# Moving GpSimd's division and the FFN layers half a step later in an attention and top-k FFN kernel

## The chip, the core and the metric

The kernel runs on one core of a Trainium2 chip. The metric is the device time of one execution in microseconds. Before the change the median of three runs is 708.19 us (706.77 to 708.98). The profile was taken in a further execution, whose span from the first to the last instruction is 704.8 us; all times within the kernel count from the start of that span.

## The reference, cut to what matters

```python
# attention: q, k, v are (8, 8, 1152, 64), float32
q_pool = q.reshape(B, H, S // 2, 2, D).mean(axis=3)          # 576 queries
scores = scale * np.matmul(q_pool, k.transpose(0, 1, 3, 2))
attn = softmax(scores)                                       # over 1152 keys
x = matmul(attn, v), heads side by side                      # (8, 576, 512)

# mixture of depths: in each batch, 128 of the 576 tokens get the FFN
scores = np.einsum('bsd,d->bs', x, w_gate)                   # the gate
out = x.copy()
for b in range(B):
    top_idx = np.argpartition(-scores[b], capacity)[:capacity]
    xe = x[b, top_idx]
    ye = np.maximum(xe @ w1, 0.0) @ w2                       # 512 -> 1024 -> 512
    g = 1.0 / (1.0 + np.exp(-scores[b, top_idx]))
    out[b, top_idx] = x[b, top_idx] + g[:, None] * ye
```

## The kernel before

The work is cut into 32 *pairs* (two heads of one batch) and each pair into two *halves* (288 of its 576 queries), so there are 64 halves, numbered 0 to 63; an even half is the first of its pair. `run` goes over the halves and emits, for each, one stretch of instructions for every engine. Each engine executes its own list strictly in the order in which it was emitted.

What one half does, engine by engine:

- TensorE (PE): `scores(h)`, 9 chunks of keys against the queries, then `weighted(h-1)`, the attention weights of the half before times v.
- ScalarE (ACT): the exponential of each chunk into `p`, the copy `two` of the weighted result, and small copies between groups of partitions.
- GpSimd (POOL): `folded` adds two thirds of `p` (three `acc` instructions), `multiplied` forms `prod` = undivided output times gate weights, `av` adds the two parts of the weighted result, `qp` pools the queries of a coming pair, and `x` is the division by the softmax sums.
- VectorE (DVE): reduces `p` and `acc` to softmax sums (`fold`, `sum`), transposes keys and queries of a coming pair (`kT`, `qT`) and the output (`avb`), takes reciprocals (`rec`), and does the ranking of the tokens.
- SyncE (SP): the loads of the coming pairs and the stores of `x`.

```python
def weighted(self, half):
    ...                                                   # 72 matmuls
    nc.scalar.copy(two[:, :, :], av[:, :, 0:n])
    nc.gpsimd.tensor_tensor(out=half["av"][:, :], in0=two[:, 0, :], in1=two[:, 1, :], op=ALU.add)

def normalized(self, pair):
    ...                                                   # for the last pair the sums are merged by TensorE
    nc.vector.reciprocal(rec[:, :], tot)
    nc.gpsimd.tensor_tensor(out=x[:, :, :], in0=pair["avb"][:, :, :], in1=rec (broadcast), op=ALU.mult)

def gated(self, half):
    nc.vector.tensor_reduce(pair["red"][:, ns], pair["prod"][:, ns, :], AX.X, ALU.add)
    if half["s"] == 1:
        nc.vector.tensor_tensor(out=pair["part"][:, pair["hp"], :], in0=pair["red"], in1=pair["rec"], op=ALU.mult)
        if pair["hp"] == self.NPAIR - 1:
            ...                                           # start the routing of this batch
```

The routing of a batch (`routed`) is a generator in pieces. A piece is emitted either in the middle of a half (`mid`, between `scores` and `weighted`) or at its end. For batch b, whose last half is 8b+7, the pieces of batches 0 to 5 lie in these halves: gate line at 8b+10, merged over partitions at 8b+11 and sent through DRAM to all partitions, ranking of the token tiles 0 and 1 at the end of 8b+13, tiles 2 and 3 at the end of 8b+14, tile 4 at the end of 8b+15, slot selection (`pick`, `index`) and the gather of 128 rows (`xe`, an indirect DMA from GpSimd) at the end of 8b+16, TensorE's transposes of `xe` (`xeT`) in the middle of 8b+18, the first FFN layer at 8b+19, the second at 8b+20, and the scatter after that. Batch 5 stops after its first layer and does the second behind the last half, as do batches 6 and 7 with more of theirs, so that TensorE has work there.

```python
for h in range(n_halves + 1):
    if h < n_halves:
        ...                                  # loads, stores
        self.scores(half)
        ...                                  # side_by_side (even) or spread (odd)
        self.units(mid=True)
        if h > 2: self.gated(halves[h - 3])
        self.folded(half)
        if h > 1: self.multiplied(halves[h - 2])
        if s == 0 and loaded: self.prepare_pair(upcoming)        # qp, kT, qT
    ...
    if h > 0:
        self.weighted(done); self.drained(done)                  # done = halves[h - 1]
    ...
    if 1 < h < n_halves and s == 0: done["pair"]["total"] = self.added(...)
    ...
    elif h > 2 and s == 1: self.normalized(halves[h - 2]["pair"])  # rec and x
    if h < n_halves: self.units(mid=False)
...                                          # behind the last half
pieces(older, self.NFC - 2)                  # older, old, new: batches 5, 6, 7
pieces(new, 1); pieces(older, 2); pieces(new, 3); pieces(older); pieces(old, self.NFC)
pieces(new, 1); ...; pieces(old, self.NFC - 3); pieces(new, 2); pieces(old); ...; pieces(new)
```

Of the kernel before, what the change touches and what calls it, by code (L numbers as in the profile page):

```python
# [10 lines left out]
P = 128  # L11
BLK = 32
# [522 lines left out]
class _Plain:  # L535
# [396 lines left out]
    def normalized(self, pair):  # L932

        nc, hp = self.nc, pair["hp"]
        tot = self.sums[:, pair["b"] * self.NPAIR + hp, :]
        if self.last_pair(pair):
            ps = self.banks()[:, 0, :]
            nc.tensor.matmul(
                ps[:, 0 : 2 * self.QB],
                lhsT=self.merge.rearrange("p g j -> p (g j)"),  # L940
                rhs=pair["sum"].rearrange("p j n -> p (j n)"),
                start=True,
                stop=True,
            )
            for j in range(2):
                rows = slice(j * self.D, (j + 1) * self.D)
                nc.scalar.activation(
                    tot[rows, :],
                    ps[rows, j * self.QB : (j + 1) * self.QB],
                    AF.Identity,  # L950
                    bias=self.tiny[rows, 0:1],
                )
        rec = pair["rec"] = self.small.tile([P, self.QB], F32, name="rec")
        nc.vector.reciprocal(rec[:, :], tot)  # L954
        x = self.work.tile([P, self.QB, BLK], F32, name="x")
        nc.gpsimd.tensor_tensor(  # L956
            out=x[:, :, :],
            in0=pair["avb"][:, :, :],
            in1=rec[:, :].unsqueeze(2).broadcast_to([P, self.QB, BLK]),
            op=ALU.mult,  # L960
        )
        pair["x"] = x

    def stored(self, pair):

# [7 lines left out]
    def gated(self, half):  # L973

        nc, pair, hb = self.nc, half["pair"], self.HB
        if half["s"] == 0:
            pair["red"] = self.small.tile([P, self.QB], F32, name="red")
        ns = slice(half["s"] * hb, (half["s"] + 1) * hb)
        nc.vector.tensor_reduce(pair["red"][:, ns], pair["prod"][:, ns, :], AX.X, ALU.add)
        if half["s"] == 1:  # L980
            nc.vector.tensor_tensor(  # L981
                out=pair["part"][:, pair["hp"], :],
                in0=pair["red"][:, :],
                in1=pair["rec"][:, :],
                op=ALU.mult,
            )
            if pair["hp"] == self.NPAIR - 1:
                unit = self.routed(pair["b"], pair["part"])
                at = next(unit) == "mid"
                self.routing.append([pair["b"], unit, at])  # L990

# [3 lines left out]
    def routed(self, b, part):  # L997
# [12 lines left out]
        sc = ffn.tile([P, NT], F32, name="gate_sc")  # L1010
        if b < self.B - 1:

            yield mid
            if b < self.B - 2:
                groups = self.side_by_side(line)
                yield True
# [19 lines left out]
                sc[0 : self.TAIL, NF:], row[NF * P :].rearrange("(t p) -> p t", p=self.TAIL)  # L1036
            )
            yield True
            if b < self.B - 2:
                yield True  # L1040
        else:

            diag = ffn.tile([P, self.QB, BLK], F32, name="diag", bufs=1)
# [34 lines left out]
        for t, rows in tiles:  # L1078
            at = t * P
            cmp = ffn.tile([P, Sp], F32, name="cmp", bufs=1)  # L1080
            own = sc[0:rows, t : t + 1]
            if t > 0:
                nc.vector.tensor_scalar(
                    out=cmp[0:rows, 0:at],
                    in0=sc_row[0:rows, 0:at],
                    scalar1=own,
                    scalar2=None,
                    op0=ALU.is_ge,
                    op1=ALU.add,
                    accum_out=parts[0:rows, t, 0:1],  # L1090
                )
            nc.vector.tensor_scalar(
                out=cmp[0:rows, at:Sp],
                in0=sc_row[0:rows, at:Sp],
                scalar1=own,
                scalar2=None,
                op0=ALU.is_gt,
                op1=ALU.add,
                accum_out=parts[0:rows, t, 1:2],
            )  # L1100
            tie = ffn.tile([P, P], F32, name="tie", bufs=1)
            nc.vector.scalar_tensor_tensor(
                out=tie[0:rows, 0:rows],
                in0=sc_row[0:rows, at : at + rows],
                scalar=own,
                in1=self.before[0:rows, 0:rows],
                op0=ALU.is_equal,
                op1=ALU.mult,
                accum_out=parts[0:rows, t, 2:3],
            )  # L1110
            if t == 1:
                yield True
            if t == 3:
                yield mid
                nc.scalar.activation(gate[:, :], gate[:, :], AF.Exp, scale=-1.0)
                if b < self.B - 2:
                    yield True
# [19 lines left out]
        for s0, w in self.slots:  # L1137
# [23 lines left out]
            else:  # L1161
# [3 lines left out]
                for of, to in ((self.token_line, found), (lines[:, :, 1, :], own_gate)):  # L1165
# [6 lines left out]
                        op1=ALU.mult,  # L1172
                        accum_out=to[0:w, :],
                    )
                nc.gpsimd.tensor_scalar(  # L1175
                    out=index[0:w, :],
                    in0=found[0:w, :],
                    scalar1=float(b * Sp),
                    scalar2=None,
                    op0=ALU.add,  # L1180
                )
            xe = ffn.tile([P, self.Dm], F32, name="xe")
            nc.gpsimd.indirect_dma_start(
                out=xe[0:w, :],
# [4 lines left out]
                oob_is_err=False,  # L1189
            )  # L1190
            yield True
            yield mid

            xeT = ffn.tile([P, self.ND, P], F32, name="xeT")
            pv = self.banks()[:, 0, :].rearrange("p (c n) -> p c n", n=P)
# [94 lines left out]
        )  # L1290
        return count_i

    def units(self, mid):


        for entry in self.routing[::-1]:
            b, unit, at = entry
            if b in self.waiting or at != mid:
                continue
            end = next((mark for mark in unit if mark), None)  # L1300
            if end is None:
                self.routing.remove(entry)
            elif end == "hidden" and b == self.B - 3:
                self.waiting.add(b)
            entry[2] = end in ("mid", "hidden") and b < self.B - 2

    def run(self):
        nc = self.nc
# [10 lines left out]
            self.load_values(loaded)  # L1319
        self.load_gate()  # L1320
        weights = self.weight_loads()
        for h in range(n_halves + 1):
            if h < n_halves:
                n, s = divmod(h, 2)
                if s == 0:
                    pair = upcoming
                    if pair["hp"] == 0:
                        part = self.ffn.tile([P, self.NPAIR, self.QB], F32, name="part")
                    pair["part"] = part
                else:  # L1330
                    loaded = None
                    if n + 2 < len(pairs):
                        loaded = self.load_pair(*pairs[n + 2])
                        self.load_values(loaded)
                    if n > 1:
                        self.stored(halves[h - 4]["pair"])
                if h > 1:
                    next(weights, None)
                half = {"pair": pair, "s": s}
                halves.append(half)  # L1340
                self.scores(half)
                if h > 1:

                    of = halves[h - 2 - s]["pair"]
                    if s == 0:
                        of["groups"] = self.side_by_side(of["sum"].rearrange("p j n -> p (j n)"))
                    else:
                        self.spread(of)
                self.units(mid=True)
                if h > 2:  # L1350
                    self.gated(halves[h - 3])
                self.folded(half)
                if h > 1:
                    self.multiplied(halves[h - 2])
                if s == 0 and loaded:
                    upcoming = loaded
                    self.prepare_pair(upcoming)
            else:
                self.stored(halves[h - 3]["pair"])
                self.gated(halves[h - 3])  # L1360
                self.multiplied(halves[h - 2])
                self.units(mid=True)
                self.units(mid=False)
            if h > 0:
                done = halves[h - 1]
                self.weighted(done)
                self.drained(done)
            if h == n_halves:
                self.multiplied(done)
                self.gated(halves[h - 2])  # L1370
            if 1 < h < n_halves and s == 0:
                done["pair"]["total"] = self.added(done["pair"]["groups"])
            if h == n_halves:
                self.normalized(done["pair"])
            elif h > 2 and s == 1:
                self.normalized(halves[h - 2]["pair"])
            if h < n_halves:
                self.units(mid=False)
        for _ in weights:
            pass  # L1380

        self.stored(halves[-1]["pair"])


        self.gated(halves[-1])
        left = [unit for _, unit, _ in self.routing]
        new = left.pop()
        old = left.pop() if left else iter(())
        older = left.pop() if left else iter(())
        assert not left  # L1390

        def pieces(unit, n=None):
            for i, _ in enumerate(unit):
                if i + 1 == n:
                    break

        pieces(older, self.NFC - 2)
        pieces(new, 1)
        pieces(older, 2)
        pieces(new, 3)  # L1400
# [71 lines left out]
```

## Time and profile before

| | value |
|---|---|
| median of 3 runs | 708.19 us (706.77 to 708.98) |
| span of the profile | 704.8 us |
| granted TensorE clock | 0.998 of full |
| score matmuls, line 818 | 4608, 295.2 us busy |
| weighted matmuls, line 836 | 4608, 294.6 us busy |
| FFN matmuls, lines 1208 and 1221 | 59.3 and 57.3 us busy |
| exponentials, line 825 | 576, 320.2 us |
| `acc` on GpSimd, line 857 | 192, 266.3 us |
| `x` on GpSimd, line 956 | 32, 37.1 us; GpSimd idle ahead of it 40.3 us |
| `part` on VectorE, line 981 | 32, 27.0 us |
| `index` on GpSimd, line 1175 | 7, 6.4 us; GpSimd idle ahead of it 20.2 us |

A group of instructions is named by its line in the program, its engine and its tile. Busy time is the time in which an engine executed; idle time ahead of a group is put down to what released it. PE is TensorE's matmuls and PEld its weight loads, which overlap.

### The profile page before, as it was taken

Reading aid. Unit: us, or ns where it says so; the run is one execution under the profiler, and the core shown is the slowest. Engines: PE = TensorE matmul, PEld = TensorE weight load, DVE = VectorE, ACT = ScalarE, POOL = GpSimd, SP = SyncE. Lnnn points to the kernel's source line nnn. Section 1 sums busy time; section 2 is a strip of 40 time slices with the busy share of each in tenths; the row PEclk is TensorE's granted clock in tenths of the full one; section 3 lists DMA queues with packets and bytes.
Section 4 is the critical chain, followed back from the end, with each engine's and each line's share of the span. In section 5 each row is a group of like instructions: output and inputs, shape, how many; then the busy total and the mean of one; then the engine's idle time right before and its main releaser. Section 6 shows DMA issues by size and latency. Waiting matters only on the chain.

```text
span 704.8 us, 23397 instructions
## 1 busy us (share of the span) xinstructions
PE 694.4 (99%) x9948; PEld 516.8 (73%) x9948; DVE 496.5 (70%) x793; ACT 444.5 (63%) x963; POOL 485.1 (69%) x452
## 2 busy tenths in 40 slices
PE   8999999999999999999999999999999999999996
PEld 5668899996758866688656887578775787766573
DVE  3877777996559965498754988559774697689540
ACT  6677778777547775477746776467754777477210
POOL 5877777868658695586955779467874877686520
PEclk9999999999999999999999999999999999999999
DMA  8888887858486483756928468382775728432200
GB/s 175 172 178 180 171 166 137 146 116 161 85 149 111 85 162 75 145 97 111 172 40 159 81 129 160 66 148 61 161 130 85 135 56 169 83 72 62 45 31 35
DMA packets 389490, 82.86 MB, mean 118 GB/s; under 512 B 376640, under 2 KB 376640, under 8 KB 389376
## 3 DMA queue, kind: packets, MB, share of 16 engines
q1 hardware_dynamic: 387872, 76.49, 58.1%
q0 software_dynamic: 1280, 4.20, 1.8%
q8 instruction: 80, 1.31, 0.8%
q10 hardware_dynamic: 224, 0.59, 0.3%
q14 instruction: 34, 0.28, 0.1%
HBM read 69.65 MB, written 11.59 MB: 115 GB/s over the span
## 4 chain that ended last, share of the span: by engine, by line
PE 89%; POOL 5%; issue 2%; DMA 1%; ACT 1%; DVE 1%; SPq 0%; POOLq 0%; DVEq 0%; ACTq 0%
PE ps L836 36%; PE ps L818 36%; PE ps L1208 8%; PE ps L1221 7%; POOL acc L857 2%; ACT p L825 1%; DMA kb<-in_k_dram 1%; DMA xe<-out_dram,index 1%; PE ps L1197 1%; POOL prod L925 1%; POOL x L956 0%; POOL av L846 0%; DVE fold L862 0%; POOL index L1175 0%; SPq L759 0%
## 5 line engine op out<-in xcount | busy, mean ns | idle before, releaser
L825 ACT ACTIVATE p<-ps 128x576 f32<-128x576 f32 x576 | 320.2, 695 | 1.7 <-PE ps L818 1.3
L818 PE MATMUL ps<-qT,kT 64*64 64x288 f32 x4608 | 295.2, 404 | 0.2 <-ACT p L825 0.2
L836 PE MATMUL ps<-p,v_sb 64*64 64x288 f32 x4608 | 294.6, 403 | 0.0
L857 POOL TENSOR_TENSOR acc<-p 128x576 f32<-128x576 f32 x192 | 266.3, 1417 | 15.4 <-ACT p L825 15.1
L836 PEld LDWEIGHTS ps<-p,v_sb 64*64 64x64 f32 x4608 | 215.5, 133 | 65.3 <-ACT p L825 9.2
L818 PEld LDWEIGHTS ps<-qT,kT 64*64 64x64 f32 x4608 | 208.0, 132 | 73.0 <-ACT p L825 15.4
L862 DVE TRANSPOSE_TENSOR_REDUCE fold<-p 128x54 f32<-128x1728 f32 x64 | 126.0, 1969 | 50.2 <-ACT p L825 50.2
L862 DVE TRANSPOSE_TENSOR_REDUCE fold<-acc 128x54 f32<-128x1728 f32 x64 | 125.3, 1957 | 46.0 <-POOL acc L857 45.8
L844 ACT COPY two<-ps 128x576 f32<-128x576 f32 x64 | 40.9, 639 | 156.9 <-PE ps L836 143.8
L846 POOL TENSOR_TENSOR av<-two 128x288 f32<-128x288 f32 x64 | 51.2, 800 | 96.5 <-ACT two L844 94.9
L915 DVE STREAM_TRANSPOSE avb<-av 128x288 f32<-128x288 f32 x64 | 29.4, 460 | 66.5 <-POOL av L846 66.5
L956 POOL TENSOR_TENSOR x<-avb,rec 128x576 f32<-128x576 f32 x32 | 37.1, 1159 | 40.3 <-DVE rec L954 27.9
L1208 PEld LDWEIGHTS ps<-xeT,w 128*128 128x128 f32 x512 | 57.8, 192 | 2.7 <-ACT p L825 2.6
L1208 PE MATMUL ps<-xeT,w 128*128 128x128 f32 x512 | 59.3, 277 | 0.0
L1221 PE MATMUL ps<-w,hT 128*128 128x512 f32 x128 | 57.3, 598 | 0.0
L925 POOL TENSOR_TENSOR prod<-avb,w_gate 128x288 f32<-128x288 f32 x64 | 51.5, 805 | 0.6 <-DVE avb L915 0.6
L902 ACT ACTIVATE sums<-total,tiny 32x18 f32<-32x18 f32 x124 | 38.1, 308 | 15.9 <-DVE total L893 14.2
L732 POOL TENSOR_TENSOR qp<-qb 128x576 f32<-128x576 f32 x31 | 43.8, 1414 | 2.2 <-DMA qb<-in_q_dram 2.2
L1221 PEld LDWEIGHTS ps<-w,hT 128*128 128x128 f32 x128 | 23.6, 190 | 28.1 <-issue 25.8
L735 DVE STREAM_TRANSPOSE kT<-kb 128x1152 f32<-128x1152 f32 x31 | 42.5, 1370 | 0.0
L887 ACT COPY groups<-sum 32x36 f32<-32x36 f32 x124 | 27.1, 219 | 6.7 <-DVE sum L872 5.2
L981 DVE TENSOR_TENSOR part<-red,rec 128x18 f32<-128x18 f32 x32 | 27.0, 845 | 1.1
(95 smaller groups left out, 290.6 us busy)
## 6 DMA issues: line engine op xcount, KB each, us to landing
kb<-in_k_dram SPq DMA_DIRECT2D x124, 144.0 KB
qb<-in_q_dram SPq DMA_DIRECT2D x124, 144.0 KB
v_sb<-in_v_dram SPq DMA_DIRECT2D x124, 144.0 KB
out_dram<-x SPq DMA_DIRECT2D x128, 72.0 KB
lines<-row_rank SPq DMA_DIRECT2D x7, 640.0 KB
w<-in_moe_w_dram SPq DMA_DIRECT2D x8, 512.0 KB
sc_row<-row SPq DMA_DIRECT2D x7, 288.0 KB
acc<-in_q_dram ACTq DMA_DIRECT2D x2, 288.0 KB
```

Source lines behind the costliest of these rows:

```text
L732: nc.gpsimd.tensor_tensor(out=qp[:, :, :], in0=pair["q"][:, :, 0, :], in1=pair["q"][:, :, 1, :], op=ALU.add)
L735: nc.vector.transpose(kT.rearrange("p (c g i) -> p c g i", c=self.NC, i=BLK), pair["k"].rearrange("p (g c) d -> p c g d", c=self.NC),)
L818: nc.tensor.matmul(sc[keys, j, 0:n], lhsT=pair["kT"][rows, c * P + keys.start : c * P + keys.stop], rhs=pair["qT"][rows, qs], start=True, ...
L825: nc.scalar.activation(p[:, c // G, c % G, :, :], sc[:, :, 0:n], AF.Exp, scale=self.scale)
L836: nc.tensor.matmul(av[j * self.D : (j + 1) * self.D, e, 0:n], lhsT=half["pair"]["v"][keys, j, c, :], rhs=half["p"][keys, c // G, c % G, j, :],
L844: nc.scalar.copy(two[:, :, :], av[:, :, 0:n])
L846: nc.gpsimd.tensor_tensor(out=half["av"][:, :], in0=two[:, 0, :], in1=two[:, 1, :], op=ALU.add)
L857: nc.gpsimd.tensor_tensor(out=acc[:, u, :], in0=units[:, 0, u, :], in1=units[:, 1, u, :], op=ALU.add)
L862: nc.vector.tensor_reduce(fold[:, a, :], of.rearrange("p u (m d) -> p (u m) d", d=BLK), AX.X, ALU.add, apply_transpose=True,)
L925: self.nc.gpsimd.tensor_tensor(out=pair["prod"][:, ns, :], in0=pair["avb"][:, ns, :], in1=self.w_gate[:, hp : hp + 1, :].broadcast_to([P, ...
L1208: nc.tensor.matmul(pv[:, f, 0:w], lhsT=self.w1[:, c, (f0 + f) * P : (f0 + f + 1) * P], rhs=xeT[:, c, 0:w], start=(c == 0), stop=(c == self ...
L1221: nc.tensor.matmul(ps[0:w, 0 : self.Dm], lhsT=hT[:, f, 0:w], rhs=self.w2[:, f, :], start=(f == 0), stop=(f == self.NFC - 1),)
```

## The change

The change moves work in time and between engines. It adds no matmul and takes none away.

1. The division `x` of a pair goes from the odd half in which its reciprocals are made to the end of the next even half (`divided`).
2. `part`, the gate sums times the reciprocals, goes from VectorE to GpSimd, except in the last two pairs of the last batch.
3. `index` goes from GpSimd to VectorE. The gather of batches 0 to 5 goes from the end of a half to a new place (`sums`) behind the `acc` instructions of the next half, and the transposes and both FFN layers follow one half later. The gate line is formed at `sums` too.
4. Batch 6: its gate line is merged in the middle of the next half, its tiles are ranked in two units (0 to 2, then 3 and 4) instead of three, its gather goes to the end of the last half, and the transposes of its rows go behind the last half.
5. `total` of an even half comes ahead of `kT` and `qT` on VectorE.
6. Behind the last half the order is new: `weighted` of the last half comes first, then the FFN of batch 5, both divisions and stores late, and the transposes of batch 6 behind five more steps of that FFN.

```diff
-        rec = pair["rec"] = self.small.tile([P, self.QB], F32, name="rec")
-        nc.vector.reciprocal(rec[:, :], tot)
-        x = self.work.tile([P, self.QB, BLK], F32, name="x")
-        nc.gpsimd.tensor_tensor(
+        pair["rec"] = self.small.tile([P, self.QB], F32, name="rec")
+        nc.vector.reciprocal(pair["rec"][:, :], tot)
+
+    def divided(self, pair):
+        x = pair["x"] = self.work.tile([P, self.QB, BLK], F32, name="x")
+        self.nc.gpsimd.tensor_tensor(
 ...
-            nc.vector.tensor_tensor(
+            ending = pair["b"] == self.B - 1 and pair["hp"] >= self.NPAIR - 2
+            engine = nc.vector if ending else nc.gpsimd
+            engine.tensor_tensor(
                 out=pair["part"][:, pair["hp"], :],
 ...
-            if t == 1:
+            cuts = (2,) if b == self.B - 2 else (1, 3)
+            if t == cuts[0] < cuts[-1]:
                 yield True
-            if t == 3:
+            if t == cuts[-1]:
                 yield mid
 ...
-                nc.gpsimd.tensor_scalar(
+                nc.vector.tensor_scalar(
                     out=index[0:w, :],
 ...
+                yield "sums" if b < self.B - 2 else True
             xe = ffn.tile([P, self.Dm], F32, name="xe")
             nc.gpsimd.indirect_dma_start(...)
             yield True
-            yield mid
+            if b < self.B - 2:
+                yield True
+            if b != self.B - 2:
+                yield mid
 ...
+            self.units("mid")
+            if h > 2:
                 self.gated(halves[h - 3])
+            self.folded(half)
+            self.units("sums")
+            if h > 1:
                 self.multiplied(halves[h - 2])
+            if h > 1 and s == 0:
+                last["total"] = self.added(last["groups"])
+            if s == 0 and loaded:
+                self.prepare_pair(upcoming)
             if h > 0:
+                self.weighted(halves[h - 1])
+                self.drained(halves[h - 1])
+            if h > 2 and s == 1:
+                self.normalized(halves[h - 2]["pair"])
+            if h > 3 and s == 0:
+                self.divided(halves[h - 3]["pair"])
+            self.units("end")
 ...
+        self.gated(halves[-3])
+        self.weighted(halves[-1])
+        self.drained(halves[-1])
+        self.multiplied(halves[-2])
+        self.multiplied(halves[-1])
+        self.gated(halves[-2])
+        pieces(older, 1)
+        self.normalized(halves[-1]["pair"])
+        for half in (halves[-3], halves[-1]):
+            self.divided(half["pair"])
+            self.stored(half["pair"])
+        self.gated(halves[-1])
+        _, new, _ = self.routing.pop()
+        pieces(new, 1)
+        pieces(older, self.NFC - 3)
+        pieces(old, 1)
         pieces(new, 1)
         pieces(older, 2)
         pieces(new, 3)
```

## The prediction, made before the result was known

> **What bounds the kernel now.** I read the page's first two parts, then TensorE's own waits, then the timeline of TensorE at the places the waits name, and last GpSimd and VectorE around those places.
>
> ```profile
> PE 694.4 (99%) x9948; PEld 516.8 (73%) x9948; DVE 496.5 (70%) x793; ACT 444.5 (63%) x963; POOL 485.1 (69%) x452
> PE   8999999999999999999999999999999999999996
> POOL 5877777868658695586955779467874877686520
> ```
>
> TensorE is busy 694.4 of 704.8 us, and the slices show where the other 10.4 us lie: in the first and in the last. No other engine passes 70%. So taking work off GpSimd or VectorE gains nothing by itself; the change can only gain where one of them makes TensorE wait. TensorE's waits, cut to the second half of the run:
>
> ```profile
> PE ps L1197 <- DMA xe<-out_dram,index: 0.6, 1, 0.6
> PE ps L1054 <- DVE rank_parts L1076: 0.4, 1, 0.4
> PE ps L1197 <- ACT p L825: 0.3, 1, 0.3
> ```
>
> They add up to 1.3 us. But busy time hides waits in a pipelined engine, so I also took the spacing between starts. A clean stretch of scores or of weighted values takes 4.37 us from its start to the start of the next. The stretch of scores ahead of the transposes (line 1197) of batches 0 to 5 takes 4.68, 4.74, 4.81, 5.33, 4.80 and 5.22 us. One of the six, in the timeline of TensorE (start, length, engine, line):
>
> ```profile
> 590.49 4.91 PE L818 MATMUL ps<-qT,kT 64*64 64x288 f32 x72
> 595.71 0.63 PE L1197 MATMUL ps<-ident,xe 128*128 128x128 f32 x4 [0.31 <-ACT p L825]
> ```
>
> A change of matmul shape costs something of itself: scores ahead of the first FFN layer (line 1208) take 4.48, so 0.11 us. Above 4.48 the six lose 0.20 + 0.26 + 0.33 + 0.85 + 0.32 + 0.74 = 2.7 us. The releaser is ScalarE: the transposes need a PSUM buffer that an exponential must first empty. In five of these six halves the copy `two` that goes ahead of the exponentials starts 0.62 to 0.77 us after the scores start, not 0.33 as elsewhere, and it starts just after GpSimd's gather instruction ends. Batch 1, in the timelines of GpSimd and ScalarE:
>
> ```profile
> 246.71 1.14 POOL L1183 DMA_INDIRECT xe<-out_dram,index  x1 [0.28 <-POOL index L1175]
> 248.16 0.64 ACT L844 COPY two<-ps 128x576 f32<-128x576 f32 x1 [2.22 <-PE ps L836]
> ```
>
> The gather ends at 247.85, `two` starts at 248.16. I don't know the mechanism; that the two belong together is my reading of a coincidence seen five times.
>
> The end, again TensorE's timeline:
>
> ```profile
> 648.00 4.59 PE L836 MATMUL ps<-p,v_sb 64*64 64x288 f32 x72
> 653.20 0.63 PE L1197 MATMUL ps<-ident,xe 128*128 128x128 f32 x4 [0.61 <-DMA xe<-out_dram,index]
> 653.76 4.59 PE L836 MATMUL ps<-p,v_sb 64*64 64x288 f32 x72
> 658.29 0.41 PE L938 MATMUL ps<-sum,merge 128*128 128x36 f32 x2
> 658.53 5.40 PE L1221 MATMUL ps<-w,hT 128*128 128x512 f32 x12
> 664.28 1.21 PE L1054 MATMUL ps<-diag,ones 128*128 128x288 f32 x4 [0.35 <-DVE rank_parts L1076]
> ```
>
> TensorE waits 0.61 us for batch 6's rows and 0.35 us for the last batch's gate line. From 664.28 on it has no gap until its last matmul at 698.2.
>
> **What the Trainium skill says.** "Perfetto Trace Analysis", section "Identifying the Most-Contended Engine", warns that busy time of pipelined matmuls is no measure of what is left. The trace agrees: 2.7 us lie in the spacing above and only 0.5 us of them show as idle time. Its section "GPSIMD Engine Instruction" advises timing GpSimd by start-to-start spacing, which I do below; the trace's `acc` at 131.09 follow each other every 4.16 / 3 = 1.39 us, against a listed mean of 1.417. "SBUF — State Buffer", section "SBUF: two separate sides", says VectorE instructions with two SBUF inputs and GpSimd exclude each other for a whole instruction. The trace agrees: the tie comparison (line 1102) lasts 271 to 1575 ns, and `part` on 18 elements takes a mean of 845 ns. So `part` costs VectorE mostly waiting, and less on GpSimd.
>
> **The change part by part.**
>
> *Removed from VectorE:* 30 of 32 `part`, 30 x 0.845 = 25 us. *Added to GpSimd:* from 805 ns for 288 elements and 1417 ns for 576, about 0.19 us plus 2.1 ns an element, so 0.23 us for 18, 30 times: 7 us. `index` takes 7 x 0.92 = 6.4 us off GpSimd. `x` no longer waits for its reciprocals (40.3 us idle ahead of it), nor `index` for `pick` (20.2 us). All of this lies beside TensorE: worth nothing directly.
>
> *The gather and the transposes.* In batches 0 to 5 the gather moves behind `acc` of half 8b+17 and the transposes to 8b+19. Rows that landed 4.9 us after the gather's start now have over 10 us, and the gather no longer lies between `weighted` and `two`. If `two` starts 0.33 us after the scores, the exponential that frees the transposes' buffer, the sixth, ends 0.33 + 0.54 + 6 x 0.545 = 4.1 us after them, before the scores end. So most of the 2.7 us goes: I take 2.2.
>
> *The end.* The transposes of batch 6 move behind 5 more FFN steps, so the last `weighted` starts at 652.4 instead of 653.76. FFN step 0 (0.86) and line 938 (0.3) follow, then 5 steps of 0.86: the transposes are due at 662.3. The gather starts when GpSimd has done `acc` of half 63 (about 653.9, below), `prod` and `av`: 655.7, and lands by 660.6. No wait. The gate line: last `two` at 656.9, `av` to 658.3, `avb`, two `prod` to 659.9 (the divisions, 1.16 us each, are no longer ahead), `red`, `part` (0.62), `line`, `diag` (0.76) at 662.2; line 1054 is due at 662.8. No wait, with 0.6 us to spare. Gain 0.61 + 0.35, plus two changes of shape of about 0.15 saved around the last `weighted` and the batch 6 merge: 1.3 us. From line 679 on the order is as before, so the gain is kept.
>
> *The new wait.* GpSimd now executes `part` of an even half ahead of `acc`, and `part` needs `red`, which stands on VectorE behind the ranking of the half before. So at halves 8b+14 and 8b+16 GpSimd can't start `acc` until the ranking is done. Batch 0, VectorE and GpSimd:
>
> ```profile
> 131.14 0.67 DVE L1092 TENSOR_SCALAR_CACHE_REDUCE cmp<-sc_row,gate_sc 128x448 f32<-128x448 f32 x1
> 131.74 0.91 DVE L1102 SCALAR_TENSOR_TENSOR tie<-sc_row,gate_sc,before 128x128 f32<-128x128 f32 x1
> 132.58 0.44 DVE L979 TENSOR_REDUCE red<-prod 128x9 f32<-128x288 f32 x1
> ...
> 131.09 4.20 POOL L857 TENSOR_TENSOR acc<-p 128x576 f32<-128x576 f32 x3
> ```
>
> Before, `acc` of half 14 started at 131.09, beside the ranking; now `part` starts at 133.1 and `acc` at 133.3, 2.2 us later. With the trace's spacings I carried this on: VectorE's second `fold` of half 14 starts at 137.5, `total` and `kT` and `qT` end at 142.1, tiles 2 and 3 (2.8 us) end at 145.1, both folds of half 15 at 149.4, tile 4 and the ranks at 151.5, `red` at 151.8, `part` and `acc` of half 16 from 151.9 to 156.2, its second `fold` to 158.3, `total`, `kT` and `qT` to 160.9. TensorE needs this `qT` at 161.96, when the scores of half 18 start. Before, it was there at 158.45. The slack falls from 3.5 to 1.1 us. It is enough, unless a tie comparison meets `acc` badly: in batch 3 one took 1.57 us instead of 0.34, which would use it up. I count 0.5 us of new waits in six batches.
>
> Sum: -2.2 - 1.3 + 0.5 = -3.0 us, 708.2 to 705.2.
>
> **Rivals.**
>
> *Hidden anyway.* TensorE is 99% busy, the long scores come from ScalarE's pace whatever GpSimd does, and one half later they are as long. For it: ScalarE needs 9 x 0.545 = 4.9 us for exponentials of scores that take 4.37, in every half. Against it: line 1208 needs a buffer in the same way and its scores take 4.48. Then only the end's 1.3 us remain: 706.9.
>
> *VectorE becomes the bound while it ranks.* If my 1.1 us of slack is 1 us too high, and ties are slow, `qT` comes up to 1.5 us late in each of six batches, at halves 18, 26, 34, 42, 50 and 58. For it: VectorE is full in these stretches (18.75 of 20 us from 140 to 160). Against it: the FFN just ahead gives it 7 us of rest in each batch. Then 6 x 1.5 = +9 less 3: 711 at worst, 708 to 709 more likely.
>
> *The end stalls on the later gather.* GpSimd's `acc` of half 63 comes behind `part` of half 62, which waits for tiles 3 and 4 of batch 6; my time of 653.9 includes this. A gather 2 us later would cost 0.3 us. Small in any case.
>
> **Range and chances.** The middle is 705.2; if the body gains nothing, 706.9; the three runs before differ by 2.2 us among themselves. Repeated small waits could bring 708.6. Everything gained and a low median give 703. A change of 2% is 14 us, more than all idle time of TensorE (10.4 us) and more than the worst rival adds, so both outer chances are small.
>
> **What will show it.** The step on the gather is right if scores ahead of line 1197 take 4.4 to 4.5 us from start to start, and wrong if they still take 4.7 to 5.3. The end is right if lines 1197 and 1054 show no wait and line 679 starts about 1.3 us nearer to the end of the last scores. The new wait is right if `acc` of half 14 starts about 2 us later against the scores than before, and harmless if the scores of halves 18 to 58 show no wait on VectorE's `qT`. The prediction fails if such waits appear in several batches, or if the late `two` has another cause than the gather.

## The result, and the profile after

The changed kernel takes 704.49 us (median of 6 runs, 704.04 to 705.81), the kernel before 707.19 us (6 runs, 706.57 to 708.98). The ratio is 0.9962 with a 95% interval of 0.9946 to 0.9977: a small gain of 2.7 us, 0.4% of the time. The prediction was 705.2 us. That the total is so close is partly luck: one term of its sum was too large by 1.0 us and another by 0.5 us the other way, and the median of the kernel before came down by 1.0 us with three more runs; so the terms are taken one at a time below.

The first part of the page, of the changed kernel:

```profile
PE 692.2 (98%) x9948; PEld 521.6 (74%) x9948; DVE 478.4 (68%) x770; ACT 446.5 (64%) x963; POOL 491.6 (70%) x475
```

VectorE is 18 us less busy: it gave up 25.7 us of `part`, but its `pick` takes 9.6 us more, as it now meets `acc` on GpSimd. GpSimd is 6.5 us busier: `part` adds 6.8, `index` takes 6.4 away, and the same 192 `acc` take 7.7 us more. TensorE has the same 9948 matmuls and is still busy nearly all the time. TensorE's waits, all of them:

```profile
PE ps L783 <- DMA kb<-in_k_dram: 1.4, 2, 1.0
PE ps L1024 <- DVE line L1010: 1.2, 1, 1.2
PE ps L612 <- POOL ones L605: 1.0, 1, 1.0
```

(Columns: us in total, times, longest.) Lines 783 and 612 belong to the start of the run, which the change doesn't touch. The transposes (line 1205, before 1197) and the gate line of the last batch (line 1056, before 1054) no longer wait. In their place stands a wait that the prediction didn't have: line 1024, the merge of batch 6's gate line, waits 1.2 us for VectorE. There is no wait on `qT`.

The groups of `part` and `x` (busy, mean ns; then the engine's idle time just before them and who ended it):

```profile
L986 POOL TENSOR_TENSOR part<-red,rec 128x18 f32<-128x18 f32 x30 | 6.8, 226 | 64.2 <-DVE red L981 56.4
L959 POOL TENSOR_TENSOR x<-avb,rec 128x576 f32<-128x576 f32 x32 | 37.2, 1162 | 0.0
```

`part` costs 226 ns on GpSimd, as estimated (0.23 us), against a mean of 845 ns on VectorE before. GpSimd's idle time moved from ahead of `x` (40.3 us before, 0.0 now) to ahead of `part` (64.2 us).

**Where the 2 us between the profiled executions lie** (span 704.8 before, 702.9 after). I cut both traces at the start of the scores of the first half, at those of half 63, at line 679 behind the last batch's gate line, and at the end:

| stretch | before | after | difference |
|---|---|---|---|
| start to scores of half 0 | 8.73 | 8.88 | +0.15 |
| scores of half 0 to scores of half 63 | 634.91 | 633.80 | -1.11 |
| scores of half 63 to line 679 | 23.50 | 22.29 | -1.21 |
| line 679 to the end | 37.7 | 37.9 | +0.2 |

The first row is the first load of k; the last row holds the same instructions in both kernels. The two middle rows are the change. Within the body, the time from the scores of half 8b+17 to those of half 8b+22, which holds the transposes and both FFN layers of batch b in both kernels, falls by 0.10, 0.19, 0.26, 0.75 and 0.25 us in batches 0 to 4, together 1.55 us, and rises by 0.38 us in batch 5 (from half 57 to half 63). The stretch of scores ahead of the transposes is where it falls; batch 1 in the changed kernel, 4.55 us from start to start, where it took 4.74:

```profile
256.31 4.62 PE L818 MATMUL ps<-qT,kT 64*64 64x288 f32 x72
260.86 0.66 PE L1205 MATMUL ps<-ident,xe 128*128 128x128 f32 x4
```

Batch 5 is where line 1024 stands, behind the scores of half 59. TensorE's timeline there (start, length, and in brackets the idle time before it and who ended it):

```profile
597.87 4.62 PE L818 MATMUL ps<-qT,kT 64*64 64x288 f32 x72
603.73 0.37 PE L1024 MATMUL ps<-line,merge 128*128 128x18 f32 x2 [1.24 <-DVE line L1010]
```

VectorE and GpSimd in the same stretch:

```profile
596.21 0.40 DVE L981 TENSOR_REDUCE red<-prod 128x9 f32<-128x288 f32 x1
...
601.06 1.98 DVE L862 TRANSPOSE_TENSOR_REDUCE fold<-acc 128x54 f32<-128x1728 f32 x1 [2.57 <-POOL acc L857]
603.32 0.27 DVE L1010 TENSOR_REDUCE line<-part 128x18 f32<-128x72 f32 x1
```

```profile
596.69 0.23 POOL L986 TENSOR_TENSOR part<-red,rec 128x18 f32<-128x18 f32 x1 [1.33 <-DVE red L981]
596.87 4.15 POOL L857 TENSOR_TENSOR acc<-p 128x576 f32<-128x576 f32 x3
```

The last `part` of batch 6 is ready at 596.92, and its gate line takes VectorE 0.27 us. But the change emits that line among the units at "sums", behind both folds of half 58. The second fold needs `acc`, which GpSimd only starts after `part` and ends at 601.0. So the line, whose data have been there for 6 us, is executed at 603.32, and TensorE reaches line 1024 first.

### The profile page after: what moved, and what is told of

Same layout as the page of the kernel before. It is cut to its first block, busy times and chain, and to the rows that moved or that the text cites. A ratio compares the mean times of both kernels' runs of the same rounds, so it can differ in the third digit from the quotient of the medians.

```text
span 702.9 us, 23365 instructions
## 1 busy us (share of the span) xinstructions
PE 692.2 (98%) x9948; PEld 521.6 (74%) x9948; DVE 478.4 (68%) x770; ACT 446.5 (64%) x963; POOL 491.6 (70%) x475
## 4 chain that ended last, share of the span: by engine, by line
PE 88%; POOL 6%; issue 3%; DVE 1%; DMA 1%; ACT 0%; SPq 0%; POOLq 0%; DVEq 0%; ACTq 0%
PE ps L836 36%; PE ps L818 35%; PE ps L1216 8%; PE ps L1229 6%; POOL acc L857 3%; DMA kb<-in_k_dram 1%; POOL av L846 1%; POOL prod L925 1%; PE ps L1205 1%; ACT p L825 0%; POOL x L959 0%; POOL qp L732 0%; DVE fold L862 0%; POOL out_dram L1254 0%; SPq L759 0%
## 5 line engine op out<-in xcount | busy, mean ns | idle before, releaser
L857 POOL TENSOR_TENSOR acc<-p 128x576 f32<-128x576 f32 x192 | 274.0, 1455 | 8.3 <-ACT p L825 8.3
L818 PEld LDWEIGHTS ps<-qT,kT 64*64 64x64 f32 x4608 | 213.3, 133 | 66.3 <-ACT p L825 6.9
L986 POOL TENSOR_TENSOR part<-red,rec 128x18 f32<-128x18 f32 x30 | 6.8, 226 | 64.2 <-DVE red L981 56.4
L1224 ACT ACTIVATE hT<-ps 128x512 f32<-128x512 f32 x16 | 9.6, 598 | 39.0 <-PE ps L1216 39.0
```

The source lines that it names most:

```text
L818: nc.tensor.matmul(sc[keys, j, 0:n], lhsT=pair["kT"][rows, c * P + keys.start : c * P + keys.stop], rhs=pair["qT"][rows, qs], start=True, ...
L857: nc.gpsimd.tensor_tensor(out=acc[:, u, :], in0=units[:, 0, u, :], in1=units[:, 1, u, :], op=ALU.add)
```

## The experiments

Two groups of four kernels, each group on one chip with its own runs of the kernel before. The theory when they were chosen: the gain comes from the gather that no longer makes `two` late and from the reordered end; the 1.24 us at line 1024 hide the rest. The rivals: the new place of the gather isn't what helps; the move of `part` costs more than it brings; the ranking already sits on the path. The first group is the two kernels with the gather back, the one with `part` on VectorE and the one with tiles ranked twice; beside it the kernel before took 706.81 us (one run). Beside the second group it took 708.04 us (median of 11). Where there is a single run, I compare spacings within the traces: between the two profiles of the changed kernel no spacing of scores differs by more than 0.06 us.

### The gather back at the end of half 8b+16

From the changed kernel, batches 0 to 5 only; the FFN stays where the change put it.

```diff
-                yield "sums" if b < self.B - 2 else True
+                if b >= self.B - 2:
+                    yield True
```

> Changed kernel with the gather of batches 0 to 5 back at the end of half 8b+16; the transposes stay in the middle of 8b+19. Theory (the gather's place makes ScalarE's copy two late): two of the halves 18, 26, ... 58 starts 0.6 to 0.8 us after the scores start in at least four of six, against 0.35 in the changed kernel; the scores ahead of the transposes stay at 4.55 us from start to start, and the total is 0 to 1 us longer. Rival (two was late because of something else that the change moved, such as the transposes or x): two stays at 0.35 us everywhere and the time is that of the changed kernel.

It took 712.22 us (span 710.5, 7.6 over the changed kernel). Neither theory had it so. The copies `two` of half 8b+18 are on time, 0.33 to 0.37 us after the scores: the gather now starts at 249.69 in batch 1, after that copy (248.93), not before it. But one half later something else is late. GpSimd, then ScalarE, in batch 1:

```profile
249.69 1.14 POOL L1189 DMA_INDIRECT xe<-out_dram,index  x1 [3.04 <-ACT two L844]
250.86 4.14 POOL L857 TENSOR_TENSOR acc<-p 128x576 f32<-128x576 f32 x3
```

```profile
257.42 0.91 ACT L887 COPY groups<-sum 32x36 f32<-32x36 f32 x4 [2.76 <-DVE sum L872]
```

GpSimd stands still for 3.04 us ahead of the gather: it executes in order, and the index comes from VectorE's `pick`. (The view names `two` as the releaser; but `two` starts at 248.93, and it is the index, which VectorE has at 249.41, that the gather reads and starts 0.28 us after.) `acc` of half 8b+17 comes late by that, the fold and `sum` after it too, ScalarE waits 2.76 us for `sum`, and the `two` ahead of the exponentials of half 8b+19 starts 0.74 to 1.07 us after the scores. The spacings of the scores add up to 0.90, 0.74, 0.74, 0.66 and 0.74 us in batches 0 to 4, and 3.78 us in batch 5, where line 1024 now waits 3.0 us. So the gather's place is worth having, but for a reason of order on GpSimd that neither side had named.

This run also shows how a late `two` reaches TensorE. Take the time from the start of the scores to the start of `two`: in batches 0 to 4 the stretch of scores ahead of the transposes lasts 3.99 us more than that each time, 5.06 us where `two` starts after 1.07 us and 4.73 us where it starts after 0.74. In batches 0, 1, 2 and 4 of the kernel before it lasts 4.06 to 4.07 us more. So the stretch grows one to one with a late `two`, whatever made it late.

### The same, with the index on GpSimd again

```diff
-                nc.vector.tensor_scalar(
+                index_on = nc.gpsimd if b < self.B - 2 else nc.vector
+                index_on.tensor_scalar(
                     out=index[0:w, :],
 ...
-                yield "sums" if b < self.B - 2 else True
+                if b >= self.B - 2:
+                    yield True
```

> As the run before, and the conversion index of batches 0 to 5 is on GpSimd again ahead of the gather. If the gather alone makes two late, this run shows the same as the one without index on GpSimd (two 0.6 to 0.8 us after the scores). If index on GpSimd is the cause, only this run shows late copies. If neither does, two is at 0.35 us in both, and the cause is elsewhere.

710.31 us (span 708.6), with the same picture: `two` is on time at half 8b+18 and starts 0.81 to 1.07 us after the scores at half 8b+19, and line 1024 waits 3.1 us. So it is the third of the three cases: the engine of `index` is not the cause, and what GpSimd waits for is `pick`.

### The gather behind `acc` in the kernel before

This one moves `index` and the gather of batches 0 to 5 behind the `acc` of half 8b+17, in the kernel before; the transposes stay at half 8b+18.

```diff
+                if b < self.B - 2:
+                    yield "sums"
                 nc.gpsimd.tensor_scalar(
 ...
-            entry[2] = end in ("mid", "hidden") and b < self.B - 2
+            entry[2] = "sums" if end == "sums" else end in ("mid", "hidden") and b < self.B - 2
 ...
                 self.folded(half)
+                self.units(mid="sums")
```

> Kernel before the change with one alteration: index and gather of batches 0 to 5 go from ahead of the acc instructions of half 8b+17 to behind them; the transposes stay in the middle of 8b+18, as do x and part. Theory (the gather's moment makes ScalarE's copy two late): two of the halves 18, 26, ... 58 starts 0.35 us after the scores start, not 0.62 to 0.77. The rows land later, so the transposes of line 1197 or so now wait 1 to 3 us for the DMA each, and the kernel is slower by 5 to 15 us. Rival (two is late for another reason, such as x, part or the transposes themselves): two still starts 0.6 us or more after the scores.

717.43 us (span 715.6). The copy `two` starts 0.35 to 0.37 us after the scores in all six batches, where five of them had 0.62 to 0.78. ScalarE and GpSimd in batch 1:

```profile
251.35 0.64 ACT L844 COPY two<-ps 128x576 f32<-128x576 f32 x1 [1.90 <-PE ps L836]
```

```profile
251.81 1.14 POOL L1185 DMA_INDIRECT xe<-out_dram,index  x1 [0.28 <-POOL index L1177]
```

The gather now starts after `two`, and `two` is on time. That supports the prediction's reading of the coincidence. The sixth batch of the kernel before, batch 3, adds to it. There `two` is not late (0.35 us), and yet the stretch lost most of all, 0.85 us. GpSimd, ScalarE and TensorE in the kernel before:

```profile
419.02 1.14 POOL L1183 DMA_INDIRECT xe<-out_dram,index  x1 [0.28 <-POOL index L1175]
419.06 0.64 ACT L844 COPY two<-ps 128x576 f32<-128x576 f32 x1 [0.82 <-PE ps L836]
419.92 0.65 ACT L825 ACTIVATE p<-ps 128x576 f32<-128x576 f32 x1 [0.22 <-PE ps L818]
420.85 4.45 ACT L825 ACTIVATE p<-ps 128x576 f32<-128x576 f32 x8 [0.28 <-PE ps L818]
421.56 2.35 PE L818 MATMUL ps<-qT,kT 64*64 64x288 f32 x32 [0.16 <-ACT p L825]
```

The gather started 0.04 us before `two`, and the two exponentials behind `two` came 0.22 and 0.28 us late instead. In all six batches the late instruction is one that waited for TensorE, and `index`, which moved together with the gather here, had ended before (at 418.74 in batch 3). In this run the gather lies over the exponentials too, and they stand still for 0.13 us at most. Why a gather under way delays another engine remains open. TensorE's wait for the rows shows the other side:

```profile
PE ps L1199 <- DMA xe<-out_dram,index: 11.5, 7, 3.3
```

Of these seven waits, the one for batch 6's rows (0.6 us) was there before. Without the FFN's move by a half the later gather costs 10.8 us (span 715.6 against 704.8), within what was expected. The two halves of the change need each other.

### The gate line of batch 6 formed right behind `part`

From the changed kernel. The gate line is VectorE's one reduction per batch; only that of batch 6 moves, from behind both folds of half 58 to ahead of them.

```diff
-                self.routing.append([pair["b"], self.routed(pair["b"], pair["part"]), "sums"])
+                unit = self.routed(pair["b"], pair["part"])
+                at = next(unit) if pair["b"] == self.B - 2 else "sums"
+                self.routing.append([pair["b"], unit, at])
```

> Changed kernel in which batch 6's gate line is formed right behind its part, ahead of both folds of half 58, instead of behind them. Theory (TensorE's 1.24 us wait at line 1024 comes from the line's place behind the folds): the line ends at about 597.5 instead of 603.6 us, line 1024 waits 0.1 us or less, and the kernel takes 1.2 us less than the changed one, ratio to the kernel before about 0.9945. Rival (the wait belongs to a PSUM buffer or to ScalarE, as that of line 1197 before): the wait stays at about 1.2 us with ScalarE as releaser and the time does not move.

703.00 us (median of 6, 702.84 to 704.71), ratio to the kernel before 0.9932 (0.9917 to 0.9947). The changed kernel unaltered was run beside it:

> The changed kernel, unaltered, on the same chip as the others, for comparison. Every theory expects its first result again: ratio to the kernel before 0.995 to 0.998.

It took 704.20 us (6 runs, 703.95 to 705.24), ratio 0.9947 (0.9933 to 0.9961); the kernel before had 708.04 us on this chip (11 runs). TensorE's waits in the kernel with the early line, all of them:

```profile
PE ps L612 <- POOL ones L605: 1.0, 1, 1.0
PE ps L783 <- DMA kb<-in_k_dram: 1.0, 2, 0.7
```

The wait at line 1024 (1026 in this kernel) is gone. VectorE ends the line 5.2 us ahead of the merge, and TensorE goes straight on:

```profile
596.46 0.28 DVE L1012 TENSOR_REDUCE line<-part 128x18 f32<-128x72 f32 x1 [0.34 <-POOL part L986]
597.39 4.61 PE L818 MATMUL ps<-qT,kT 64*64 64x288 f32 x72
601.93 0.40 PE L1026 MATMUL ps<-line,merge 128*128 128x18 f32 x2
```

Of all spacings between scores just one differs from the changed kernel's by more than 0.08 us: that of half 59, by -1.21. This is the missed term; by the medians of six runs the kernel is 1.20 us faster than the changed one beside it.

### `part` back on VectorE

```diff
-            engine = nc.vector if ending else nc.gpsimd
+            engine = nc.vector
```

> Changed kernel with part on VectorE in all pairs. Theory (part on GpSimd holds acc behind VectorE's ranking): GpSimd's acc of half 16 starts about 2 us earlier against the scores, its idle time ahead of part (64 us) is gone, and the wait of line 1024 for the gate line of batch 6 falls from 1.24 us to under 0.3 us; span about 701.7 us against 702.9. Rival (part on VectorE costs VectorE 25 us where it is short of time): waits of the scores on qT appear in halves 18 to 58, and the span is 704 or more.

736.10 us (span 734.3). The theory has its first step right: `acc` of half 16 starts 3.3 us after the scores instead of 7.4. But the wait at line 1024 grows instead of shrinking, and the kernel gets slower. The rival has the kind right, waits on `qT` (at halves 28, 36 and 52), but not the size. The group, TensorE's two longest waits, and one case on VectorE and on GpSimd:

```profile
L986 DVE TENSOR_TENSOR part<-red,rec 128x18 f32<-128x18 f32 x32 | 58.3, 1821 | 1.1
```

```profile
PE ps L818 <- DVE qT L739: 15.2, 3, 5.1
PE ps L1024 <- DVE line L1010: 8.0, 1, 8.0
```

```profile
254.74 9.85 DVE L986 TENSOR_TENSOR part<-red,rec 128x18 f32<-128x18 f32 x1
```

```profile
252.34 4.13 POOL L857 TENSOR_TENSOR acc<-p 128x576 f32<-128x576 f32 x3
...
259.31 1.15 POOL L959 TENSOR_TENSOR x<-avb,rec 128x576 f32<-128x576 f32 x1
260.43 4.12 POOL L857 TENSOR_TENSOR acc<-p 128x576 f32<-128x576 f32 x3
```

A multiplication of 18 elements stood on VectorE for 9.85 us, and ended at 264.59, when GpSimd's run of back-to-back instructions ended (260.43 + 4.12 = 264.55). It can't be its own work: nine of the 32 `part` of this run met no GpSimd instruction, and took 178 to 180 ns. The Trainium skill's page "SBUF — State Buffer", section "SBUF: two separate sides", says that a GpSimd instruction that reads SBUF and a VectorE instruction with two SBUF inputs exclude each other, each for a whole instruction. The trace agrees and goes further: VectorE lost not one round but the last `acc`, `prod`, `qp`, `av`, `x` and the three `acc` after it, eight GpSimd instructions in a row after the one in progress.

This is the exception, not the rule. Four of the 32 `part` waited so (9.85 to 9.88 us, 39 of the 58.3 us). The other 19 that met GpSimd took 0.2 to 1.8 us and got in when one or two of its instructions had ended, though GpSimd went on without a pause. In the kernel before, 27 of 32 got in so at the first end, as this one between the second and the third of the three `acc` at 131.09:

```profile
133.05 0.89 DVE L981 TENSOR_TENSOR part<-red,rec 128x18 f32<-128x18 f32 x1
```

So it was not GpSimd's rests that let `part` through before. What decides who goes next isn't shown, nor whether it is the move of `x`, of the gather or something else in the change that matters. Four of the six batches pay: the spacing behind the scores of half 8b+19 grows by 5.2 to 5.3 us in batches 1, 2 and 4, with 1.4 to 2.2 us more a half later, and by 9.1 us in batch 5; batches 0 and 3 got through.

### Tiles 2 and 3 ranked twice

From the changed kernel, batches 0 to 5: the loop body over a tile is executed twice for t = 2 and 3. The second pass writes the same values.

```diff
         for t, rows in tiles:
+            for _ in range(2 if t in (2, 3) and b < self.B - 2 else 1):
```

> Changed kernel in which batches 0 to 5 rank their tiles 2 and 3 twice (same output), some 3 us more on VectorE in half 8b+14. Theory (qT of half 8b+18 has 1.3 us to spare, and nothing in between gives way): the scores of halves 18, 26, ... 58 wait 1.5 to 2.2 us each, 9 to 13 us in all, span 712 to 716. Rival (VectorE's rests take it up): no wait, span 703.

717.54 us (span 715.7, 12.8 over the changed kernel), inside the theory's range. VectorE's `qT` of half 16 and TensorE's scores of half 18, first of this kernel, then of the changed one:

```profile
162.85 0.72 DVE L739 STREAM_TRANSPOSE qT<-qp 128x576 f32<-128x576 f32 x1
163.72 4.60 PE L818 MATMUL ps<-qT,kT 64*64 64x288 f32 x72 [1.27 <-ACT two L844]
```

```profile
160.15 0.72 DVE L739 STREAM_TRANSPOSE qT<-qp 128x576 f32<-128x576 f32 x1
162.16 4.64 PE L818 MATMUL ps<-qT,kT 64*64 64x288 f32 x72
```

The extra ranking delays `qT` by 2.70 us, and the scores by 1.56. The difference, 1.14, plus a hand-over of 0.15 us (163.72 - 163.57) is the slack of the changed kernel: 162.16 - 160.87 = 1.29 us there (1.30 to 1.34 in the other batches). The spacing of the scores grows by 1.51 to 1.55 us in five batches, by 2.95 in batch 5, and by 2.7 us at half 59 (line 1024), 13.3 in all. The releaser named at the wait is `two`, but it is `qT` that moved.

### The division of pair 30 ahead of the two last gate products

```diff
         self.drained(halves[-1])
+        self.divided(halves[-3]["pair"])
         self.multiplied(halves[-2])
 ...
         for half in (halves[-3], halves[-1]):
-            self.divided(half["pair"])
+            if half is halves[-1]:
+                self.divided(half["pair"])
             self.stored(half["pair"])
```

> Changed kernel in which, behind the last half, the division of pair 30 is ahead of the two gate products on GpSimd again. Theory (at the end the gate line of batch 7 hangs on GpSimd's order, with 0.15 us to spare at line 1056): line 1056 waits 0.9 to 1.1 us for VectorE, and what follows comes that much later; span 703.9 us against 702.9. Rival (hidden, as five FFN steps run on TensorE there): no wait, span unchanged.

706.41 us in a single run (span 704.6). Two things ahead of the altered part made it longer: the first scores started 0.65 us later and took 0.53 us more, and in batch 0 `pick` lost two more rounds to `acc` on GpSimd, so that the gather came 2 us late and the scores 0.29 us. The program is the same as the changed one up to there:

```profile
162.31 3.86 DVE L1169 SCALAR_TENSOR_TENSOR pick<-lines,token,token_line 128x640 f32<-128x640 f32 x1
```

So I take only the end. From the scores of half 63 to line 679 it takes 22.87 us instead of 22.29, and TensorE shows the wait that the change removed, a little shorter than expected:

```profile
PE ps L1056 <- DVE rank_parts L1078: 0.7, 1, 0.7
```

The two `prod` come 1.1 us later, and the end gets 0.58 us longer. The missing half lies in `diag`, the last step on VectorE ahead of line 1056; first this kernel, then the changed one:

```profile
663.17 0.76 DVE L1046 TENSOR_TENSOR diag<-line,same 128x576 f32<-128x576 f32 x1
```

```profile
660.61 1.35 DVE L1046 TENSOR_TENSOR diag<-line,same 128x576 f32<-128x576 f32 x1
```

In the changed kernel `diag` runs beside the two `x` on GpSimd (659.08 to 661.35) and takes 1.35 us; here it starts when the last `x` has ended (662.80). Line 1056 starts 0.15 us after `diag` ends in both kernels (661.96 to 662.11, and 663.93 to 664.08). So the changed kernel has no time to spare there, although the profile shows no wait.

## Why the prediction was right, and where it was off

**The gather and the transposes (2.2 us): right in mechanism, 1.1 us of it eaten by a wait that was missed.** The scores ahead of the transposes take 4.55 us from start to start in batches 0 to 4, where they took 4.68 to 5.33. (The criterion was "4.4 to 4.5". The change of shape had been sized from another line; but with the tiles ranked twice the same stretch takes 4.50, so shape alone doesn't explain the rest.) That gives 1.55 us, half of it, 0.75, in batch 3. There the prediction's account doesn't fit as it stands: not `two` was late but the exponentials behind it; it is still the gather that lay over them. In batch 5 the stretch takes 5.86 us instead of 5.22. With the early gate line this last loss turns into a gain, and the body becomes 632.53 us, 2.38 shorter than before: 2.2 was about the right size of the step, but it holds for a kernel whose line 1024 doesn't wait. The step that failed is "the batch 6 merge", which was counted as part of a saving of 0.15 us in matmul shape: it costs a wait of 1.24 us. The prediction didn't ask behind which other work VectorE would come to the gate line.

**The new wait (0.5 us): none.** The step of carrying the trace's spacings on held to 0.5 us: `acc` of half 14 starts at 132.80 (133.3 predicted; against the scores 1.5 us later than before, where the criterion said about 2), `qT` of half 16 ends at 160.87 (160.9), the slack is 1.29 us (1.1). No batch used it up. The rival "VectorE becomes the bound while it ranks" was the dangerous one; ranking twice shows that it begins 1.1 us further on (1.29 less the hand-over).

**The end (1.3 us): 1.21.** Both waits are gone. The step "with 0.6 us to spare" was mis-sized: `diag` was taken at 0.76 us and takes 1.35 us, since the divisions that were moved away from ahead of `prod` now run beside it. What was spare is used up, but no more than that.

**`part` ("lies beside TensorE: worth nothing directly"): wrong in kind.** With everything else of the change made and `part` left on VectorE, the kernel's span is 31.4 us longer than the changed one's. The prediction had priced each part alone, against the kernel before. Its reading that `part` costs VectorE "mostly waiting" is right: 178 ns of work in a mean of 845, and 226 ns on GpSimd. (Of the tie comparisons that it quotes, 271 ns is the smaller shape, 64x64; the 128x128 ones take 0.33 to 1.57 us.)

**The rival "hidden anyway" (706.9)** falls with the measured 4.55 us and the 632.53 us of the early line.

The sum by its terms: -1.55 (gather, batches 0 to 4) + 0.38 (batch 5) = -1.17 from the spacings, which the cut of the body has as -1.11; -1.21 (end); +0.3 at the two ends of the run, which the change doesn't touch; together -2.0. The medians differ by 2.7 us.

**What stays open.** Why the gather under way delays ScalarE by some 0.3 us: its place is shown to matter, its mechanism isn't. How VectorE and GpSimd decide who goes next, and which of the moves makes `part` on VectorE so dear, was not tried beyond the runs above.

## What to carry to other kernels

A change made of several moves has to be priced as a whole: `part` looked worthless alone, and leaving it out makes the changed kernel 31 us longer. A small two-input instruction on VectorE beside a busy GpSimd mostly waits for one instruction, but now and then for a whole run of them; where TensorE hangs on what follows it, the rare case sets the time. When a piece is merged "in the next half", look at what stands ahead of it in its engine's list, and not just at when its data are ready; moving one reduction of 0.27 us ahead of two folds was worth 1.2 us. And spacings from start to start, carried on step by step, foretold a slack of 1.3 us to within 0.2 us; idle times alone would not have shown it.

## What the runs showed of the hardware that I had not expected

- A VectorE instruction with two SBUF inputs waited 9.85 us through an unbroken run of nine GpSimd instructions; 4 of 32 waited so long. Beside none it takes 178 to 180 ns; the mean of all 32 is 1821 ns, and on GpSimd the same work takes 226 ns.
- Larger instructions that meet both become longer. In the changed kernel, `pick` now meets `acc` on GpSimd: it takes 1.14 and 1.91 us in batch 0 instead of 0.86 and 0.89, and the three `acc` 5.32 us instead of 4.15. TensorE shows no wait for it. In the run with the division ahead, the first of the two took 3.86 us in batch 0.

```profile
162.34 1.91 DVE L1169 SCALAR_TENSOR_TENSOR pick<-lines,token 128x640 f32<-128x640 f32 x1
160.21 5.32 POOL L857 TENSOR_TENSOR acc<-p 128x576 f32<-128x576 f32 x3
```

- An indirect gather of 1.14 us on GpSimd that is under way when a stretch of matmuls ends goes with a ScalarE copy of the result that starts 0.62 to 0.78 us after the next scores instead of 0.35 (five batches). Where the copy had just begun, the two exponentials behind it came 0.22 and 0.28 us late (one batch).
